# Fused forgetting attention and MLP: score tiles ahead of AV runs in batch 0, and two x transposes of batch 1 through the DMA crossbar

## The chip, the cores and the metric

The kernel runs on one core of a Trainium2 chip. The metric is the device time in microseconds of one execution. Engines are named as in the profile: PE is TensorE (PEld its weight loads), DVE is VectorE, ACT is ScalarE, POOL is GpSimd, SP is SyncE. An engine's queue is written with a q behind it: SPq issues DMAs only.

## The reference

Attention with a forget gate over 8 batches, 8 heads, 576 tokens and a head size of 64, followed by a two-layer MLP with exact GELU. All inputs and the output are float32.

```python
scores = (1 / sqrt(D)) * q @ k.T                       # per batch and head
cum    = cumsum(log(clip(f, 1e-4, 1)))                 # along the tokens
scores = where(causal, -1e9, scores + cum[:, None] - cum[None, :])
attn   = softmax(scores)
x      = (attn @ v)  -> transposed to [4608 tokens, 512]   # heads side by side
h      = x @ w_in                                      # 512 -> 2048
out    = (0.5 * h * (1 + erf(h / sqrt(2)))) @ w_out    # 2048 -> 512
```

## The kernel before

**Data.** Heads go in four pairs per batch (`HP = 4`). For each pair, `qT` and `kT` hold q and k with the 64 features of two heads on 128 partitions and 576 tokens along the free axis. The decay is folded into v: `weigh_v` (L267) multiplies v by a weight per key token (`wT`) and writes `vw` in bf16; a 65th column of weights gives the softmax's denominator. One call is one pair.

**Score tiles.** `scores(b, i, t)` (L283) computes one of four score tiles of pair i, transposed (keys on partitions), in a PSUM buffer of the pool `s_psum` (two buffers), and ScalarE exponentiates it into `e` (L313). In batch 0 and for pair 0 of batch 1 TensorE also adds the causal mask; otherwise GpSimd zeroes the masked part of `e` (L315). `attend` (L327) is an AV run: per head 15 matmuls of `e` with `vw` into an `o_psum` or `m_psum` buffer (two of each). `normalize` (L342) divides by the denominator on VectorE and writes x, tokens on partitions.

**From x to GEMM1.** GEMM1 wants x with features on partitions (`xT`). There are two ways. `to_xT` (L360) makes five TensorE transposes into PSUM and one copy by VectorE or ScalarE. `x_dma` (L372) is one DMA transpose through the crossbar, issued on SP. Before the change, batches 0 and 1 use `to_xT` for all four pairs, and later batches `x_dma`.

**From q and k to qT and kT.** Batches 0 and 1 use TensorE (`transposes_first`, L203: twelve transposes into PSUM, then a copy). Later batches use the crossbar: `transpose_dma` (L229) issues one transpose for q and one for k over four heads on SP, and `untangle` (L244) puts the result into `qT` and `kT` with eight VectorE copies a pair (L253). Batch 2's are issued in the middle of batch 1, when its q and k have landed.

**Order.** All instructions are placed by hand (`manual_schedule`): each engine runs its own in the order of the program, waits on semaphores, and nothing is reordered. `first_attention` (L581) writes out batch 0, `second_attention` (L746) batch 1, in which GEMM1 blocks that batch 0 left over (`gemm1_hold`) and the first part of GEMM2 of batch 0 (`take(fill, n)`) are put between the attention's pieces. After each attention follow GEMM1 of that batch (L819 on; there `untangle` of the next batch is put between) and, mixed into the next attention, GEMM2 in row halves (`gemm2_second` L544, `gemm2_rows` L473: PSUM banks of the pool `o_psum`, named "o", and of `m_psum`, named "m"; VectorE adds the partial sums at L561 and L513). `gemm1_begin` (L667) is the start of GEMM1 of batches 0 and 1.

**Queues.** Loads of q, k and weights, which are cast to bf16, are issued on GpSimd and stand in one order with its weighing (L272) and masking (L315). Loads of v stand on GpSimd in batches 0 and 1 and on SP later, where they share the order with crossbar transposes and stores of the output. GpSimd takes a DMA's semaphore again only when the DMA that had it eight issues before has landed.

**Batch 0 around the change.** Pair 0's v is weighed by VectorE in two instructions: key blocks 0 to 3, then block 4. The copy of `kT` of pair 3 is held back until after that (`late=True`). AV runs start as early as their operands allow: pair 0's stands ahead of score tile (2, 3), and in two stretches, row blocks 0 to 3 for both heads, then row block 4. The three w_in quarters are issued on GpSimd behind the last load of v, and GpSimd weighs pairs 2 and 3 behind them.

Of the kernel before, what the change touches and what calls it, by code (L numbers as in the profile page):

```python
# [20 lines left out]
NBLK = 5  # L21
# [32 lines left out]
def kernel(  # L54
# [10 lines left out]
    nc = tc.nc  # L65
# [25 lines left out]
    o_psum = ctx.enter_context(tc.tile_pool(name="o_psum", bufs=2, space=PSUM))  # L91
# [77 lines left out]
    def load_w_in(c):  # L169
        f4 = slice(c * d_ff // 4, (c + 1) * d_ff // 4)  # L170
        nc.gpsimd.dma_start(w_in_sb[:, :, f4], w_in_r[:, :, f4])
# [28 lines left out]
    tails = consts.tile([P, n_dm, TC], BF16)  # L200


    def transposes_first(b, i, which, pool, tag, late=False):  # L203

        src = qk_of[b][which]
        ps = pool.tile([P, JT, PT], BF16, tag=tag, name="ps_f")
        for j in range(JT):
            for h in range(2):
                nc.tensor.transpose(  # L209
                    ps[h * D : (h + 1) * D, j, :],  # L210
                    src[:, 2 * i + h, j * D : (j + 1) * D],
                    ident_bf[:PT, :PT],
                )

        dst = (qT, kT)[which][i].rearrange("d (p j) -> d p j", j=JT)
        src = ps.rearrange("d j p -> d p j")
        if late:
            return partial(nc.vector.tensor_copy, dst, src)
        if b or i:
            nc.vector.tensor_copy(dst, src)  # L220
        elif which:
            nc.vector.tensor_copy(dst[:, 0 : PT // 2], src[:, 0 : PT // 2])
            nc.scalar.copy(dst[:, PT // 2 :], src[:, PT // 2 :])
        else:
            nc.scalar.copy(dst, src)

    tq_of = {}

# [38 lines left out]
    def weigh_v(b, i, eng=nc.gpsimd, n0=0, n1=NBLK):  # L267

        hs = slice(2 * i, 2 * i + 2)
        bh = b * H + 2 * i  # L270
        w = wT[:, n0:n1, bh : bh + 2].rearrange("p n h -> p h n")
        eng.tensor_tensor(  # L272
            vw(b)[:, hs, n0:n1, 0:D],
            v_sb[:, hs, n0:n1, :],
            w.unsqueeze(3).to_broadcast([P, 2, n1 - n0, D]),
            Alu.mult,
        )
        if b:
            eng.tensor_copy(vw(b)[:, hs, :, D], w)
# [47 lines left out]
    def attend(b, i, h, ms, pool=o_psum, tag="o"):  # L327
        if (b, i, h) not in o_of:
            o_of[b, i, h] = pool.tile([P, NBLK, D + 1], FP32, tag=tag, name="o")
        o = o_of[b, i, h]  # L330
        for m in ms:
            for n in range(m + 1):
                t, c = where(n, m)
                nc.tensor.matmul(  # L334
                    o[:, m, :],
                    e_of[b, i, t][:, h, c : c + P],
                    vw_of[b][:, 2 * i + h, n, :],
                    start=(n == 0),
                    stop=(n == m),
                )  # L340

    def normalize(b, i, h):  # L342
        if (b, i) not in x_of:
            x_of[b, i] = x_pool.tile([P, NBLK, 2, D], BF16, tag="x", name="x")
        o = o_of[b, i, h]
        r = x_pool.tile([P, NBLK], FP32, tag="r", name="r")
        nc.vector.reciprocal(r, o[:, :, D])  # L347
        nc.vector.tensor_tensor(  # L348
            x_of[b, i][:, :, h, :],
            o[:, :, 0:D],  # L350
            r.unsqueeze(2).to_broadcast([P, NBLK, D]),
            Alu.mult,
        )
# [227 lines left out]
    def first_attention():  # L581


        def transposes(i, pool, tag):
            transposes_first(0, i, 0, pool, tag)
            transposes_first(0, i, 1, pool, tag)

        def attend_head(i, h, *at):
            attend(0, i, h, (0, 1, 2, 3, 4), *at)
            normalize(0, i, h)  # L590

        warm_up(9)
        transposes(0, o_psum, "o")
        nc.vector.tensor_tensor_scan(
            decay[:, S - 2 :: -1],
            f_sb[:, S - 1 : 0 : -1],
            none[:, 0 : S - 1],
            2.0**80,
            Alu.mult,
            Alu.add,  # L600
        )
        warm_up(2, 2 * P)
        scores(0, 0, 0)
        scores(0, 0, 1)
        transposes_first(0, 1, 0, m_psum, "m")
        scores(0, 0, 2)
        transposes_first(0, 1, 1, m_psum, "m")
        psw = o_psum.tile([P, NBLK, BH], FP32, tag="o", name="psw")
        for n in range(NBLK):
            nc.tensor.transpose(  # L610
                psw[:, n, :], decay[:, K0[n] : K0[n] + P], ident_fp[:BH, :BH]
            )
        scores(0, 0, 3)
        nc.vector.tensor_copy(wT[:, 0:4, :], psw[:, 0:4, :])
        nc.vector.tensor_copy(wT[D:P, 4, :], psw[D:P, 4, :])
        nc.vector.tensor_copy(
            vw(0)[:, :, :, D], wT[:, :, 0:H].rearrange("p n h -> p h n")
        )
        scores(0, 1, 0)
        transposes_first(0, 2, 0, m_psum, "m")  # L620
        scores(0, 1, 1)
        transposes_first(0, 2, 1, m_psum, "m")
        scores(0, 1, 2)
        scores(0, 1, 3)
        transposes_first(0, 3, 0, m_psum, "m")
        scores(0, 2, 0)
        copy = transposes_first(0, 3, 1, m_psum, "m", late=True)
        weigh_v(0, 0, nc.vector, 0, NBLK - 1)
        weigh_v(0, 0, nc.vector, NBLK - 1)
        copy()  # L630
        weigh_v(0, 1, nc.vector)
        load_w_in(0)
        load_w_in(1)
        load_w_in(2)
        weigh_v(0, 2)
        weigh_v(0, 3)
        load_qk_tokens(1, 0, 4)
        nc.gpsimd.memset(v_sb[:, :, 0, 0:1], 0.0)
        load_v(1, 0, 4, nc.gpsimd)
        load_w_in(3)  # L640
        load_qk_tokens(1, 4, 8)
        load_v(1, 4, 8, nc.gpsimd)
        scores(0, 2, 1)
        scores(0, 2, 2)
        for ms in ((0, 1, 2, 3), (4,)):
            for h in range(2):
                attend(0, 0, h, ms)
        for h in range(2):
            normalize(0, 0, h)
        scores(0, 2, 3)  # L650
        scores(0, 3, 0)
        for h in range(2):
            attend_head(1, h, m_psum, "m")
        scores(0, 3, 1)
        scores(0, 3, 2)
        for h in range(2):
            attend_head(2, h)
        scores(0, 3, 3)
        to_xT(0, 0, nc.vector.tensor_copy)
        to_xT(0, 1, nc.scalar.copy)  # L660
        attend_head(3, 0)
        both = s_psum.tile([P, 2, 1024], BF16, tag="s", name="ps_x2")
        to_xT(0, 2, nc.scalar.copy, ps=both[:, 0, 0:XC])
        attend_head(3, 1)
        gemm1_begin(0, both)

    def gemm1_begin(b, both):  # L667
# [78 lines left out]
    def second_attention():  # L746


        b, fill = 1, gemm2_first(0)

        def av(i, h):
            attend(b, i, h, (0, 1, 2, 3, 4))
            normalize(b, i, h)

        def transposes(i, pool, tag):
            for which in range(2):
                transposes_first(b, i, which, pool, tag)


        nc.scalar.activation(warm[0:1, 0:1], warm[0:1, 0:1], Act.Exp)  # L760
        def tiles(i, t):
            scores(b, i, t)
            scores(b, i, t + 1)

        def run(i):
            av(i, 0)
            av(i, 1)

        tiles(0, 0)
        transposes(1, o_psum, "o")  # L770
        gemm1_hold(10)
        gemm1_hold(11)
        tiles(0, 2)
        gemm1_hold(12, nc.scalar.copy)
        transposes(2, o_psum, "o")
        tiles(1, 0)
        gemm1_hold(13)
        run(0)
        tiles(1, 2)
        gemm1_hold(14, nc.scalar.copy)  # L780
        transposes(3, o_psum, "o")
        weigh_v(1, 2)
        tiles(2, 0)
        gemm1_hold(15)
        run(1)
        weigh_v(1, 3)
        tiles(2, 2)
        take(fill, 4)
        tiles(3, 0)
        transpose_dma(2, 0, 4)  # L790
        transpose_dma(2, 4, 8)
        to_xT(b, 0, nc.vector.tensor_copy, o_psum, "o")
        to_xT(b, 1, nc.vector.tensor_copy, o_psum, "o")
        take(fill, 4)
        tiles(3, 2)
        behind(qk_of[2][1], H - 1)
        load_w_out(2)
        load_w_out(3)
        run(2)
        take(fill, 4)  # L800
        av(3, 0)
        take(fill, 4)
        both = s_psum.tile([P, 2, 1024], BF16, tag="s", name="ps_x2")
        to_xT(b, 2, nc.scalar.copy, ps=both[:, 0, 0:XC])
        av(3, 1)
        gemm1_begin(1, both)
        x_tail(1)
        load_v(2)

    for b in range(B):  # L810
# [8 lines left out]
        for ffb in range(4 if b < 2 else 5, n_ff):  # L819
# [17 lines left out]
            elif b + 1 < B:  # L837
                first, gap = (5, 3) if b == 1 else (1, 4)
                at, late = divmod(ffb - first, gap)
# [40 lines left out]
```

## Time and profile before

The median of three runs is 335.3 us (334.8 to 336.39).

| | |
|---|---|
| profiled execution | 337.87 us |
| its span | 335.9 us |
| PE busy | 325.7 us (97%) |
| ACT busy | 206.6 us (61%) |
| DVE busy | 184.2 us (55%) |
| POOL busy | 133.0 us (40%) |
| granted PE clock | 1.0 throughout |
| chain that ended last | PE 90%, DMA 4%, POOL 2% |
| DMA engines busy, first 75 us | 80% or more in each slice |

How to read it: a line of a timeline is start in us, length in us, engine, line of the program, operation, and "out<-in" by names, with the number of instructions merged into it; in square brackets stands the idle time of that engine just ahead of it and what ended it. The chain is followed back from the last instruction, at each step to what released it; "issue" is time for which the profile shows no wait. A line of the DMA view's third part is queue and kind, packets, megabytes, and the time that the packets took as a share of 16 DMA engines (packets of several queues overlap, so shares above 100% occur). q0 carries the DMAs that GpSimd issues, q1 those of SP, q8 TensorE's program.

The stages, by the timeline: batch 0's attention until about 26 us, its GEMM1 until 35, batch 1's attention until 56, its GEMM1 until 70, and from 70 us on batch 2 to 7, each attention mixed with GEMM2 of the batch before.

### The profile page before, as it was taken

To read this page: it belongs to the slowest core of one execution; us is meant where nothing else is said; L and a number is where in the kernel's file an instruction comes from. 1 tells how busy PE (TensorE), PEld (TensorE's weight loads), DVE (VectorE), ACT (ScalarE), POOL (GpSimd) and SP (SyncE) were. 2 spreads that over 40 slices of the span, in tenths; PEclk is the share of its full clock that TensorE was granted. 3 is DMA by queue.
4 is the path that set the end of the run, shared out by engine and by line. 5 is a ranking of instruction groups with operands and counts; after the bars stand their busy time and mean duration, and the time that the engine had idled before them with its cause. 6 is when DMAs were issued, how large, how long until landed. Compare 5 with 4: busy or idle time off the path is not lost.

```text
span 335.9 us, 7819 instructions
## 1 busy us (share of the span) xinstructions
PE 325.7 (97%) x3161; PEld 170.7 (51%) x3161; DVE 184.2 (55%) x424; ACT 206.6 (61%) x298; POOL 133.0 (40%) x260
## 2 busy tenths in 40 slices
PE   7779999999999999999999999999999999999995
PEld 3564555445554456445644555446544654444443
DVE  5671666594358945894579547964696550020011
ACT  4957886983734787378827882788378846404600
POOL 8787874029437044723445344525441420000000
PEclk9999999999999999999999999999999999999999
DMA  8999998999998799599947995769800231011012
GB/s 117 188 187 219 194 189 116 158 181 158 207 205 175 120 204 185 102 140 149 212 128 108 170 195 157 112 119 192 195 13 2 87 72 49 0 72 54 0 45 81
DMA packets 97427, 44.16 MB, mean 131 GB/s; under 512 B 75728, under 2 KB 92368, under 8 KB 97392
## 3 DMA queue, kind: packets, MB, share of 16 engines
q1 hardware_dynamic: 79344, 27.55, 41.6%
q0 software_dynamic: 17648, 15.60, 30.5%
q8 instruction: 24, 0.39, 0.5%
q10 hardware_dynamic: 400, 0.52, 0.4%
q14 instruction: 11, 0.09, 0.1%
HBM read 36.85 MB, written 9.44 MB: 138 GB/s over the span
## 4 chain that ended last, share of the span: by engine, by line
PE 90%; DMA 4%; POOL 2%; issue 1%; DVE 1%; ACT 0%; POOLq 0%; ACTq 0%
PE ps L389 36%; PE ps L493 26%; PE o L334 9%; PE ps L433 8%; PE s L303 7%; DMA v_sb<-in_v_dram 2%; DMA xT<-x 1%; PE ps L553 1%; PE ps_x L367 1%; PE ps L529 1%; PE ps_f L209 1%; POOL k L109 1%; POOL q L109 1%; DVE vw L272 0%; ACT e L313 0%
## 5 line engine op out<-in xcount | busy, mean ns | idle before, releaser
L409 ACT ACTIVATE g<-ps 128x512 bf16<-128x512 f32 x138 | 78.5, 601 | 79.8 <-PE ps L389 79.3
L313 ACT ACTIVATE e<-s 128x896 bf16<-128x896 f32 (+2 forms) x128 | 100.2, 835 | 23.8 <-PE s L303 18.7
L389 PE MATMUL ps<-xT,w_in_sb 128*128 128x512 bf16 x512 | 113.6, 379 | 0.1
L493 PE MATMUL ps<-w_out_sb,g 64*128 64x512 bf16 (+1 forms) x711 | 108.0, 377 | 0.0
L389 PEld LDWEIGHTS <-w_in_sb 128*128 128x128 bf16 x576 | 55.5, 98 | 67.4 <-issue 3.1
L315 POOL TENSOR_SCALAR_AFFINE_SELECT e<-e 128x256 bf16<-128x256 bf16 (+1 forms) x135 | 49.1, 383 | 90.1 <-ACT e L313 89.9
L493 PEld LDWEIGHTS <-g 64*128 64x128 bf16 (+1 forms) x711 | 39.4, 95 | 34.7 <-issue 4.2
L272 POOL TENSOR_TENSOR vw<-v_sb,wT 128x640 bf16<-128x640 f32 x30 | 38.7, 1290 | 26.1 <-DMA v_sb<-in_v_dram 15.3
L303 PE MATMUL s<-qT,kT 64*128 64x320 bf16 (+4 forms) x384 | 42.9, 276 | 1.5 <-ACT e L313 0.7
L253 DVE COPY kT<-tk 64x288 bf16<-64x288 bf16 x96 | 42.8, 446 | 1.6
L253 DVE COPY qT<-tq 64x288 bf16<-64x288 bf16 x96 | 40.0, 417 | 5.1 <-DMA tq<-q 3.7
L334 PEld LDWEIGHTS <-e 128*128 128x128 bf16 x960 | 34.7, 98 | 9.6 <-POOL e L315 2.9
L501 DVE COPY ot<-ps 128x512 f32<-128x512 f32 x20 | 13.8, 692 | 46.5 <-PE ps L493 46.5
L334 PE MATMUL o<-vw,e 128*128 128x65 bf16 x960 | 37.1, 194 | 1.3 <-DVE vw L272 1.3
L348 DVE TENSOR_TENSOR x<-o,r 128x320 bf16<-128x320 f32 x64 | 31.5, 492 | 3.1 <-DVE r L347 0.7
L442 DVE COPY ot<-ps 128x512 f32<-128x512 f32 (+2 forms) x9 | 5.7, 632 | 49.6 <-PE ps L433 49.6
L303 PEld LDWEIGHTS <-kT 64*128 64x128 bf16 x384 | 19.2, 94 | 21.5 <-issue 4.8
L433 PE MATMUL ps<-w_out_sb,g 128*128 128x512 bf16 (+2 forms) x144 | 28.0, 355 | 0.0
L433 PEld LDWEIGHTS <-g 128*128 128x128 bf16 x144 | 13.5, 98 | 14.5
L347 DVE RECIPROCAL r<-o 128x5 f32<-128x5 f32 x64 | 12.1, 188 | 11.3 <-PE o L334 11.3
L513 DVE TENSOR_TENSOR ot<-ot,ps 128x512 f32<-128x512 f32 x22 | 15.1, 685 | 1.1
L389 PE MATMUL ps<-tails,w_in_sb 128*128 128x512 bf16 x64 | 14.3, 378 | 0.0
(69 smaller groups left out, 153.6 us busy)
## 6 DMA issues: line engine op xcount, KB each, us to landing
out_dram<-ot SPq DMA_DIRECT2D x32, 256.0 KB, 2.4
v_sb<-in_v_dram SPq DMA_DIRECT2D x24, 256.0 KB, 4.8
q<-in_q_dram POOLq DMA_DIRECT2D x6, 576.0 KB, 6.3
k<-in_k_dram POOLq DMA_DIRECT2D x6, 576.0 KB, 8.4
w_in_sb<-in_moe_w_in_dram POOLq DMA_DIRECT2D x4, 512.0 KB, 8.0
w_out_sb<-in_moe_w_out_dram POOLq DMA_DIRECT2D x4, 512.0 KB, 9.2
v_sb<-in_v_dram POOLq DMA_DIRECT2D x13, 128.0 KB, 7.1
v_sb<-in_v_dram SPq DMA_DIRECT2D x9, 128.0 KB, 4.7
```

Of the source, the lines that this page charges most:

```text
L253: nc.vector.tensor_copy(rows[:, odd], src[odd * D : (odd + 1) * D, 2 * i + h].rearrange("d j p -> d p j"),)
L272: eng.tensor_tensor(vw(b)[:, hs, n0:n1, 0:D], v_sb[:, hs, n0:n1, :], w.unsqueeze(3).to_broadcast([P, 2, n1 - n0, D]), Alu.mult,)
L303: nc.tensor.matmul(to, *ab, start=half < 0, stop=half == 1 or not masked)
L313: nc.scalar.activation(et[:, :, z:c], st[:, :, z:c], Act.Exp, scale=scale)
L315: nc.gpsimd.affine_select(out=et[:, :, c0 + z : c0 + P], in_=et[:, :, c0 + z : c0 + P], compare_op=Alu.is_ge, fill=0.0, base=z, pattern=[[ ...
L334: nc.tensor.matmul(o[:, m, :], e_of[b, i, t][:, h, c : c + P], vw_of[b][:, 2 * i + h, n, :], start=(n == 0), stop=(n == m),)
L348: nc.vector.tensor_tensor(x_of[b, i][:, :, h, :], o[:, :, 0:D], r.unsqueeze(2).to_broadcast([P, NBLK, D]), Alu.mult,)
L389: nc.tensor.matmul(ps, w_in_sb[:, kt, ffb * P : (ffb + 1) * P], src[:, kt, 0:TC], start=(kt == 0), stop=(kt == n_dm - 1),)
L409: nc.scalar.activation(g_of[c][ffb], ps, Act.Gelu)
L433: nc.tensor.matmul(pss[ts][:, c0:c1], g_of[c][kt][:, ts * P : (ts + 1) * P], w_out_sb[:, kt, c0:c1], start=(kt == 0), stop=(kt == n_ff - 1),)
L493: nc.tensor.matmul(banks[r], g_of[c][kt][rows, ts * P : (ts + 1) * P], w_out_sb[rows, kt, :], start=kt == (steps.index("r") if r else 0), ...
L513: nc.vector.tensor_tensor(ot, ot, bank, Alu.add)
```

## The change

In batch 0:

- the first qT copy is shared by VectorE and ScalarE as the first kT copy is, instead of ScalarE alone;
- the copy of kT of pair 3 is no longer held back;
- pair 0's v is weighed by GpSimd in one instruction, behind the issue of w_in quarter 0 and ahead of the issue of quarters 1 and 2;
- score tiles (2, 3), (3, 1) and (3, 3) stand ahead of the AV runs of pairs 0, 1 and 2 instead of behind them, and pair 0's AV run goes head by head in one stretch, with its `normalize` behind each head;
- xT of pair 0 is copied by ScalarE instead of VectorE;
- the second head of pair 3's AV run stands ahead of the transposes of pair 2's x instead of behind them.

In batch 1:

- x of pairs 0 and 1 goes through `x_dma`, right behind the AV run of each, instead of `to_xT` later (ten TensorE transposes and two VectorE copies). On SP the two stand ahead of batch 2's `transpose_dma`.

```diff
-    def transposes_first(b, i, which, pool, tag, late=False):
+    def transposes_first(b, i, which, pool, tag):
...
-        if late:
-            return partial(nc.vector.tensor_copy, dst, src)
         if b or i:
             nc.vector.tensor_copy(dst, src)
-        elif which:
+        else:
             nc.vector.tensor_copy(dst[:, 0 : PT // 2], src[:, 0 : PT // 2])
             nc.scalar.copy(dst[:, PT // 2 :], src[:, PT // 2 :])
-        else:
-            nc.scalar.copy(dst, src)
...
-        copy = transposes_first(0, 3, 1, m_psum, "m", late=True)
-        weigh_v(0, 0, nc.vector, 0, NBLK - 1)
-        weigh_v(0, 0, nc.vector, NBLK - 1)
-        copy()
+        transposes_first(0, 3, 1, m_psum, "m")
+        load_w_in(0)
+        weigh_v(0, 0)
         weigh_v(0, 1, nc.vector)
-        load_w_in(0)
         load_w_in(1)
         load_w_in(2)
         weigh_v(0, 2)
...
         scores(0, 2, 1)
         scores(0, 2, 2)
-        for ms in ((0, 1, 2, 3), (4,)):
-            for h in range(2):
-                attend(0, 0, h, ms)
+        scores(0, 2, 3)
         for h in range(2):
-            normalize(0, 0, h)
-        scores(0, 2, 3)
+            attend_head(0, h)
         scores(0, 3, 0)
+        scores(0, 3, 1)
         for h in range(2):
             attend_head(1, h, m_psum, "m")
-        scores(0, 3, 1)
         scores(0, 3, 2)
+        scores(0, 3, 3)
         for h in range(2):
             attend_head(2, h)
-        scores(0, 3, 3)
-        to_xT(0, 0, nc.vector.tensor_copy)
+        to_xT(0, 0, nc.scalar.copy)
         to_xT(0, 1, nc.scalar.copy)
         attend_head(3, 0)
+        attend_head(3, 1)
         both = s_psum.tile([P, 2, 1024], BF16, tag="s", name="ps_x2")
         to_xT(0, 2, nc.scalar.copy, ps=both[:, 0, 0:XC])
-        attend_head(3, 1)
         gemm1_begin(0, both)
...
         gemm1_hold(13)
         run(0)
+        x_dma(b, 0)
         tiles(1, 2)
...
         gemm1_hold(15)
         run(1)
+        x_dma(b, 1)
         weigh_v(1, 3)
         tiles(2, 2)
         take(fill, 4)
         tiles(3, 0)
         transpose_dma(2, 0, 4)
         transpose_dma(2, 4, 8)
-        to_xT(b, 0, nc.vector.tensor_copy, o_psum, "o")
-        to_xT(b, 1, nc.vector.tensor_copy, o_psum, "o")
         take(fill, 4)
```

## The prediction

> **What bounds the kernel now.** I read the page first, then the chain of waits piece by piece from 20 to 60 us, the timelines of SP, VectorE and TensorE around the two places of the edit, and last the DMA view in short windows. The page says that TensorE is busy nearly throughout:
>
> ```profile
> PE 325.7 (97%) x3161; PEld 170.7 (51%) x3161; DVE 184.2 (55%) x424; ACT 206.6 (61%) x298; POOL 133.0 (40%) x260
> ```
>
> So only what lengthens TensorE's own work or makes it wait counts; from 57 us on the chain is TensorE without a gap, and what is lost or won before that reaches the end undiminished. The chain in order of time (start, length, what) shows the two places that the edit touches:
>
> ```profile
> 22.79 0.17 PE ps_x L367 x3
> 22.96 1.62 issue
> 24.58 0.27 PE ps_x L367 x2
> ...
> 49.99 0.66 PE ps_x L367 x10
> ```
>
> The 0.66 us at 49.99 are the ten transposes of x of pairs 0 and 1 of batch 1, on the path. The 1.62 us of "issue" stand in the middle of five transposes, with no data to wait for. The DMA view tells more: a queue of kind "instruction" moves 16 KB packets, one per about 252 matmuls and weight loads of TensorE (25 for 6322). Packet times put one at 14.3 us and the next at 22.1 us, and TensorE stops after its 702nd such instruction. Counting back 252, it passed the previous boundary at 17.15 us, in the first AV run. I read this as: passing a boundary asks for the next block but one, and here it came 7.4 us later (4.95 us until its packet started, 0.9 us for it, 1.6 us after it).
>
> SP's and VectorE's timelines show a second clock, that of the DMA:
>
> ```profile
> 50.35 1.36 SPq L239 DMA_TRANSPOSE tq<-q  x1
> 53.24 1.31 SPq L239 DMA_TRANSPOSE tk<-k  x1
> 54.59 2.13 SPq L239 DMA_TRANSPOSE tq<-q  x1
> 56.76 6.73 SPq L239 DMA_TRANSPOSE tk<-k  x1
> ```
>
> ```profile
> 67.07 1.34 DVE L253 COPY qT<-tq 64x288 bf16<-64x288 bf16 x4 [3.68 <-DMA tq<-q]
> 71.13 1.34 DVE L253 COPY kT<-tk 64x288 bf16<-64x288 bf16 x4
> 72.51 0.69 DVE L561 TENSOR_TENSOR ot<-ot,ps 128x512 f32<-128x512 f32 x1
> 73.23 0.69 DVE L513 TENSOR_TENSOR ot<-ot,ps 128x512 f32<-128x512 f32 x1
> ```
>
> ```profile
> 74.23 1.89 PE L493 MATMUL ps<-w_out_sb,g 64*128 64x512 bf16 x16
> ```
>
> Batch 2's q and k are transposed by the crossbar once they have landed (50.35 and 53.24). VectorE sits idle 3.68 us until the third of these transposes has landed (67.07), untangles until 72.47, and only then adds up the first GEMM2 sums, until 73.92. That frees the two "o" banks that TensorE takes at 74.23. The margin is 0.31 us.
>
> **Part A: batch 0.** The first qT copy moves from one ScalarE copy (0.64 us) to halves on VectorE (0.46) and ScalarE (0.40). In the trace the second half of the first kT copy waits for the first half; if both pairs do so, the first exponential starts about 0.16 us later, or 0.2 earlier if not. ScalarE's 0.22 us gap at 14.69, set by k's landing, takes that: zero.
>
> kT of pair 3 (VectorE, 0.75 us) goes ahead of the weighing, into idle time: zero.
>
> The weighing of pair 0 goes from VectorE (0.69 + 0.30 us, done at 16.99) to GpSimd (1.28 us by its row). It waits for the last of pair 0's v, which VectorE saw at 16.69, so it ends at 17.97. Behind it on GpSimd stand the issues of w_in quarters 1 and 2, then at 15.79 and 16.95, now near 18.0 and 18.75; then the weighings of pairs 2 and 3 (18.53 to 21.05, now 19.5 to 22.0) and batch 1's loads (20.99, now 22.0). The packets of w_in quarter 0 end at 19.25 and a quarter's data start 1.4 us after its issue, so quarter 1 starts at 19.4: the DMA stream hardly breaks, and the gates that follow (27.10 to 30.34 us, all on landings) stay.
>
> TensorE had pair 0's AV at 16.33 to 17.3; it now does the score tile (2,3) first, waits about 1.9 us, and runs AV at 18.0 to 19.0. ScalarE's exponentials, which ended at 22.25, then end near 22.85: tile (3,0) comes 1 us later than before, and the tiles that now run ahead of AV make good most of it. Copying xT of pair 0 on ScalarE (0.69) for VectorE (0.48) makes ScalarE's two copies end at 24.2 instead of 22.9, still before GEMM1 reads them. So TensorE reaches the block boundary, now in the last AV run of pair 3, at about 23.8 instead of 22.7. From there the work is the same (12 AV matmuls and 5 transposes for 15 and 2).
>
> What decides is when the block comes. The boundary before it, passed in the same AV run, is passed 1.6 us later, at 18.75. With the same 7.4 us the block is there at 26.2, 1.6 us later than before. If the request meets a shorter queue, since w_in quarters 1 and 2 are issued later, there is no stall, and TensorE goes on at 23.8: 0.8 us earlier. Part A: -0.8 to +1.6 us. The other latencies from boundary to packet, up to 57 us, were 4.1, 3.6 (from the end of the stall), 1.1, 3.1 and 1.7 us, so I take neither end, but +0.4.
>
> [...]
>
> One more cost of moving the weighing: pair 1's weighing stays on VectorE (0.82 us) and waits for the same v. What the two engines do to each other shows where GpSimd weighs beside untangling:
>
> ```profile
> 102.49 1.79 DVE L253 COPY qT<-tq 64x288 bf16<-64x288 bf16 x2
> ```
>
> Two copies that take 0.67 us elsewhere take 1.79 here: one waited for GpSimd. If GpSimd waits instead, AV starts 0.82 us later, w_in too, and the DMA stream breaks for up to 0.8 us. I count zero and keep 0.8. [...]
>
> **Part B: batch 1.** Removed are ten transposes (0.66 us of the path) and two VectorE copies (0.89 us, not on the path). What follows on TensorE then waits for exponentials that end at 51.14 instead of starting late, so I count -0.5.
>
> Added are two crossbar transposes on SP. They are ahead of batch 2's four on that queue; the second can go once x of pair 1 is normalized, 48.72, so SP itself is free again at 49.95, before 50.35. The transfers are not free:
>
> ```profile
> q0 software_dynamic: 1316, 1.00, 130.0%
> ```
>
> That is the DMA view from 45 to 50 us: the 16 engines are full with batch 2's q and k, the loads that release the transposes. One x has 128 x 640 x 2 bytes, 640 packets of 256 bytes. Their price alone and in a mix, from the windows 264 to 266 us (x by itself) and 61 to 65 us (transposes beside w_out):
>
> ```profile
> q1 hardware_dynamic: 672, 0.16, 36.4%
> ```
>
> ```profile
> q0 software_dynamic: 616, 0.61, 91.2%
> q1 hardware_dynamic: 613, 0.16, 31.5%
> ```
>
> 0.364 x 16 x 2 us / 672 = 17 ns a packet; 0.315 x 16 x 4 / 613 = 33 ns. So one x costs each engine 640/16 x 17 to 33 ns, 0.7 to 1.3 us, and two 1.4 to 2.6 us. Above that, transposes stick in busy queues: of those begun at 86.5 us many end only at 88.2, 1.7 us later, all at once. With 1.5 us of this each the two cost 5.6. I take 2.6, the mix being the nearest row. If the later load (k, 53.24) lands that much later, so does everything behind it on SP and VectorE: the untangling starts at 69.7, the sums are added by 76.5, and TensorE gets its banks 2.3 us after 74.23. If VectorE frees them after TensorE is ready, TensorE's own shift (0.4 - 0.5 = -0.1) does not matter: the later one sets the time. v of batch 2 lands at 76.1 instead of 73.5; GpSimd's chain to the AV run at 81.7 has moved by as much as TensorE.
>
> **Sum.** max(-0.1, 2.6 - 0.31) = +2.3 us. The profiled execution took 337.87 us (span 335.9), 2.6 above the median of 335.3; I carry the difference over: 335.3 + 2.3 = 337.6 us.
>
> **Rivals.**
> 1. Not slower: the transposes hide. If x of pair 0 is through before the last loads and the slowest of the 16 engines is not one that it slows, k lands as before, and the untangling's margin lets TensorE gain 0.31 at most where part A helps, while a late block leaves 1.6 - 0.5 = +1.1. For it: k's last two engines land at 53.1, 1.5 us behind the others. Against: every engine gets its share of a transpose. It decides below a delay of 0.3 us. 335.0 to 336.4 us.
> 2. Faster: the block comes before it is wanted, and q and k of batch 2 come earlier as well: -0.8 - 0.5 = -1.3 us or a little more, 333.6 to 334.0. Nothing in the profile shows what would bring them earlier.
> 3. x itself is late: x of pair 1, issued at 48.75, must land by 55.4 for GEMM1 of batch 1. With the slowest landing of an x (4.8 us) it is there at 53.6; with the slowest of a transpose in the mix (11.3 us) at 60.05, and TensorE waits 4.6 us: 339.9. For it: 130% load at the time.
>
> **How the numbers follow.** About 0.5% (1.7 us) is what a measurement of this kernel can tell from no change. The forecast's case 0.55, of which 0.45 lie above 1.7 us (own range 336.6 to 339.0); rival 1 0.25; rival 2 0.08, nearly all of it inside 1.7 us but for what is unknown; rival 3 0.12, above. So slower 0.57, within 0.36, faster 0.07. Eight in ten: from 335.0 (rival 2 and the lower edge of rival 1 left out) to 340.2 (rival 3 taken in, the 5.6 us of sticking left out).
>
> **What would show it.** Right: tq of batch 2 issued after 51 us, tk after 54.5, VectorE's idle time before L253 longer and ending near 69.7, and a wait of TensorE at L493 for VectorE's L513 near 74 us. For part A: weighing by GpSimd until 18.0 to 18.8, an "issue" gap of 1 to 3 us inside pair 3's AV run, or none. Wrong: tk issued at 53.2 as before, or TensorE waiting near 55 us for xT from DMA. The forecast falls if the two transposes take less than 0.3 us from the loads, or if the block fetch moves by more than 2 us.

## The result, and the profile after

The changed kernel takes 338.8 us (median of six runs, 338.24 to 339.95), the kernel before beside it 335.29. The ratio is 1.0101, with a 95% interval of 1.0078 to 1.0124: 3.5 us slower. The profiled execution took 338.24 us with a span of 336.5 us. Most lines of the new file stand four below those of before: the AV run is now L330, the weighing L268, untangling L249, the sums L557 and L509, GEMM2's row halves L489.

The page of the changed kernel: busy times, granted clock, and the chain by engine.

```profile
PE 323.0 (96%) x3110; PEld 171.9 (51%) x3151; DVE 182.5 (54%) x420; ACT 206.7 (61%) x299; POOL 135.8 (40%) x261
...
PEclk9979999999999999999999999999999999999998
...
PE 74%; DMA 13%; POOL 7%; DVE 2%; issue 2%; SPq 0%; ACT 0%; POOLq 0%; ACTq 0%
```

Three things are new. The granted clock has a 7 in its third slice (16.8 to 25.2 us), where it was full before. The chain no longer is TensorE from 57 us on: 13% of it are DMA now. And the "issue" stall of 1.62 us, which the prediction let decide part A, is gone.

**Batch 0.** GpSimd's, TensorE's and ScalarE's timelines of the changed kernel:

```profile
15.70 1.93 POOL L268 TENSOR_TENSOR vw<-v_sb,wT 128x640 bf16<-128x640 f32 x1 [0.71 <-DMA v_sb<-in_v_dram]
```

```profile
17.68 1.81 PE L330 MATMUL o<-vw,e 128*128 128x65 bf16 x30 [1.51 <-POOL vw L268]
```

```profile
20.34 3.27 ACT L309 ACTIVATE e<-s 128x896 bf16<-128x896 f32 x4 [3.21 <-PE s L299]
```

The weighing took 1.93 us, not the 1.28 of its row. TensorE waited 1.51 us for it, and then its AV run took 1.81 us, where the same 30 matmuls took 1.11 in the first profile of the kernel before, behind a gap of 1.14 us:

```profile
16.33 1.11 PE L334 MATMUL o<-vw,e 128*128 128x65 bf16 x30 [1.14 <-DVE vw L272]
```

Here are the windows of that stretch in the changed kernel; the last three columns are the granted clock, the DMA share and GB/s:

```profile
16.00:17.00 1.00, 0.16 (x6) 0.11 (x2) 0.49 (x1) 1.00 (x2) 1.00 (x1) 1.00 0.71 105
17.00:18.00 1.00, 0.32 (x7) 0.32 (x7) 0.00 (x0) 0.12 (x1) 1.00 (x2) 0.50 1.21 196
18.00:19.00 1.00, 1.00 (x23) 1.00 (x20) 0.27 (x2) 0.00 (x0) 1.00 (x2) 0.50 1.16 193
19.00:20.00 1.00, 1.00 (x19) 0.83 (x18) 0.86 (x3) 0.00 (x0) 0.99 (x2) 0.50 0.49 82
20.00:21.00 1.00, 1.00 (x27) 0.75 (x23) 0.24 (x1) 0.66 (x1) 1.00 (x2) 0.79 1.16 183
```

While TensorE stood, its granted clock went down to 0.5 and stayed there until 20.4 us. ScalarE, which lives from the score tiles, idled 3.21 us. By its busy share, 1.00 from 18 to 20 us, this TensorE at a clock of 0.50 looks like any busy TensorE; the clock column tells it, and the length of its rows (1.81 us instead of 1.11).

**Batch 1.** SP's and VectorE's timelines, and the chain in order of time:

```profile
44.31 6.00 SPq L369 DMA_TRANSPOSE xT<-x  x2
51.06 2.07 SPq L235 DMA_TRANSPOSE tq<-q  x1
54.72 1.42 SPq L235 DMA_TRANSPOSE tk<-k  x1
```

```profile
67.17 1.35 DVE L249 COPY qT<-tq 64x288 bf16<-64x288 bf16 x4 [2.63 <-DMA tq<-q]
...
73.35 0.69 DVE L509 TENSOR_TENSOR ot<-ot,ps 128x512 f32<-128x512 f32 x1
```

```profile
40.43 14.28 DMA k<-in_k_dram
...
56.19 10.96 DMA tq<-q
...
73.35 0.70 DVE ot L509
74.05 0.04 issue
74.09 3.66 PE ps L489 x31
```

The chain now runs from k's landing through the crossbar's tq to VectorE's untangling and sums, and TensorE joins it at 74.09, where the predicted gate stands. By how much it gates could not be read from these two profiles: the first profile of the kernel before was itself 2.6 us longer than its median.

### The profile page after: what moved, and what is told of

It is laid out like the page before. It is cut to its first block, busy times and chain, and to the rows that moved or that the text cites. A ratio compares the mean times of both kernels' runs of the same rounds, so it can differ in the third digit from the quotient of the medians.

```text
span 336.5 us, 7764 instructions
## 1 busy us (share of the span) xinstructions
PE 323.0 (96%) x3110; PEld 171.9 (51%) x3151; DVE 182.5 (54%) x420; ACT 206.7 (61%) x299; POOL 135.8 (40%) x261
## 4 chain that ended last, share of the span: by engine, by line
PE 74%; DMA 13%; POOL 7%; DVE 2%; issue 2%; SPq 0%; ACT 0%; POOLq 0%; ACTq 0%
PE ps L385 28%; PE ps L489 25%; PE ps L429 8%; PE o L330 7%; DMA k<-in_k_dram 7%; PE s L299 5%; DMA tq<-q 3%; POOL v_sb L121 2%; POOL vw L268 2%; DMA v_sb<-in_v_dram 1%; DMA xT<-x 1%; POOL q L109 1%; DVE kT L249 1%; DVE qT L249 1%; POOL k L109 1%
## 5 line engine op out<-in xcount | busy, mean ns | idle before, releaser
L385 PE MATMUL ps<-xT,w_in_sb 128*128 128x512 bf16 x495 | 112.3, 379 | 1.2 <-DMA xT<-x 0.2
L489 PE MATMUL ps<-w_out_sb,g 64*128 64x512 bf16 (+1 forms) x692 | 104.8, 376 | 1.7 <-issue 1.3
L489 PEld LDWEIGHTS <-g 64*128 64x128 bf16 (+1 forms) x711 | 40.2, 95 | 34.8 <-issue 4.7
L268 POOL TENSOR_TENSOR vw<-v_sb,wT 128x640 bf16<-128x640 f32 x31 | 40.6, 1313 | 26.6 <-PE s L299 16.0
L249 DVE COPY kT<-tk 64x288 bf16<-64x288 bf16 x96 | 46.0, 480 | 3.3 <-DMA tk<-k 1.7
L299 PE MATMUL s<-qT,kT 64*128 64x320 bf16 (+4 forms) x384 | 44.2, 278 | 2.1 <-ACT e L309 1.5
L330 PEld LDWEIGHTS <-e 128*128 128x128 bf16 x960 | 35.1, 99 | 9.6 <-issue 3.0
L330 PE MATMUL o<-vw,e 128*128 128x65 bf16 x960 | 37.5, 195 | 2.3 <-POOL vw L268 1.5
L249 DVE COPY qT<-tq 64x288 bf16<-64x288 bf16 x96 | 36.7, 382 | 4.0 <-DMA tq<-q 2.6
L299 PEld LDWEIGHTS <-kT 64*128 64x128 bf16 x384 | 20.0, 94 | 22.4 <-issue 6.1
L509 DVE TENSOR_TENSOR ot<-ot,ps 128x512 f32<-128x512 f32 x22 | 15.1, 685 | 1.1
```

Source lines behind the costliest of these rows:

```text
L249: nc.vector.tensor_copy(rows[:, odd], src[odd * D : (odd + 1) * D, 2 * i + h].rearrange("d j p -> d p j"),)
L268: eng.tensor_tensor(vw(b)[:, hs, n0:n1, 0:D], v_sb[:, hs, n0:n1, :], w.unsqueeze(3).to_broadcast([P, 2, n1 - n0, D]), Alu.mult,)
L299: nc.tensor.matmul(to, *ab, start=half < 0, stop=half == 1 or not masked)
L330: nc.tensor.matmul(o[:, m, :], e_of[b, i, t][:, h, c : c + P], vw_of[b][:, 2 * i + h, n, :], start=(n == 0), stop=(n == m),)
L385: nc.tensor.matmul(ps, w_in_sb[:, kt, ffb * P : (ffb + 1) * P], src[:, kt, 0:TC], start=(kt == 0), stop=(kt == n_dm - 1),)
L489: nc.tensor.matmul(banks[r], g_of[c][kt][rows, ts * P : (ts + 1) * P], w_out_sb[rows, kt, :], start=kt == (steps.index("r") if r else 0), ...
```

## The experiments

All were timed in five rounds. Ratios are to the kernel before, with 95% intervals.

**1. The kernel before, once more** (e0_before_again; no edit).

> The kernel before, unchanged, for a second profile of it. Its first profiled execution took 337.87 us, 2.6 us above the median of its runs, so that profile may hold stalls that most executions do not have. If so (theory S), the new profile is near 335.3 us, the 1.62 us of 'issue' inside x's transposes near 23 us is gone or much shorter, and the DMA packets that stood still from 58.8 to 60.85 us do not. If the 2.6 us are only what profiling adds (theory P), the same stalls show and the execution again takes about 338 us.

Measured: 335.61 us, 1.0013 [0.9997, 1.0029]; span of the profile 333.7 us. The 1.62 us stall isn't in it: TensorE's timeline has no "issue" gap from 14 to 27 us, and the third slice of GEMM1 began at 23.89 us instead of 26.43. SP's and VectorE's timelines of this run, in which the sums are done at 71.5 and TensorE waits for neither:

```profile
52.19 2.43 SPq L239 DMA_TRANSPOSE tk<-k  x1
```

```profile
64.64 1.34 DVE L253 COPY qT<-tq 64x288 bf16<-64x288 bf16 x4 [1.18 <-DMA tq<-q]
```

So the stall belonged to one execution, and this profile (span 333.7, 335.64 us) is the one to compare with.

**2 and 3. Each part alone.** e1_batch0_alone is the changed kernel with batch 1 as before; e2_batch1_alone is the kernel before with

```diff
         run(0)
+        x_dma(b, 0)
...
         run(1)
+        x_dma(b, 1)
...
-        to_xT(b, 0, nc.vector.tensor_copy, o_psum, "o")
-        to_xT(b, 1, nc.vector.tensor_copy, o_psum, "o")
```

> The changed kernel with batch 1 as before (x of pairs 0 and 1 of batch 1 by TensorE, two VectorE copies): part A alone. Theory B (the loss is the crossbar's, in batch 1): within 0.4 us of the kernel before. Theory A (the loss is batch 0's: the first AV run waits for GpSimd's weighing, TensorE idles 1.5 us, the granted clock falls to 0.5 for some 3 us, and the block of program that came late in the first profile of the kernel before is not late in most executions): 2.5 to 4 us slower, with part B worth -0.6 to +1.

> The kernel before with the two crossbar transposes of x in batch 1 instead of ten TensorE transposes and two VectorE copies: part B alone. Theory B, as predicted: +2.3 us or more, with VectorE untangling batch 2's later half 2 us later and TensorE waiting for VectorE's sums near 74 us. Theory A: between -0.6 us (what TensorE saves) and +1 us.

Measured: part A alone 337.89 us, 1.0077 [1.0051, 1.0104], 2.6 us; part B alone 336.55 us, 1.0049 [1.0024, 1.0075], 1.2 us. Together 3.8, and the whole change costs 3.5. The medians nearly add, but the interval of the whole change, 2.6 to 4.2 us, begins where part A alone stands; and in the profiles batch 2's first AV run starts at 79.19 us in experiment 1, at 81.93 with part A, 80.45 with part B and 81.59 with both, so there both cost no more than part A. Part A's profile shows the same late weighing, with VectorE's weighing beside it, and then the AV run:

```profile
15.88 0.83 DVE L268 TENSOR_TENSOR vw<-v_sb,wT 128x640 bf16<-128x640 f32 x1 [0.70 <-DMA v_sb<-in_v_dram]
15.92 1.93 POOL L268 TENSOR_TENSOR vw<-v_sb,wT 128x640 bf16<-128x640 f32 x1 [1.35 <-DMA v_sb<-in_v_dram]
```

```profile
17.89 1.81 PE L330 MATMUL o<-vw,e 128*128 128x65 bf16 x30 [1.79 <-POOL vw L268]
```

VectorE's weighing of pair 1 waits for v as well, starts 0.04 us earlier and takes its usual time; GpSimd's takes 0.65 us more than its 1.28. VectorE's operation still had 0.79 us to run when GpSimd's began, so the extra 0.65 us are nearly what GpSimd would lose by waiting for it. That it waits is read from these rows; what the two engines share, a port in the expectations below, no run shows. Which of the two starts first is called the race from here on.

Part B's SP, VectorE and TensorE timelines:

```profile
41.98 6.05 SPq L373 DMA_TRANSPOSE xT<-x  x2
50.07 1.80 SPq L239 DMA_TRANSPOSE tq<-q  x1
53.54 2.12 SPq L239 DMA_TRANSPOSE tk<-k  x1
```

```profile
66.05 1.35 DVE L253 COPY qT<-tq 64x288 bf16<-64x288 bf16 x4 [0.95 <-DMA tq<-q]
```

```profile
53.91 0.81 PE L389 MATMUL ps<-xT,w_in_sb 128*128 128x512 bf16 x3 [0.54 <-DMA xT<-x]
...
72.24 0.37 PE L493 MATMUL ps<-w_out_sb,g 64*128 64x512 bf16 x1 [0.18 <-DVE ot L561]
72.96 1.88 PE L493 MATMUL ps<-w_out_sb,g 64*128 64x512 bf16 x15 [0.35 <-DVE ot L513]
```

Against experiment 1, k's transpose is issued 1.35 us later and the untangling starts 1.41 us later. TensorE then waits 0.18 us for one bank at L493 and 0.35 for the other. Ahead of the banks it is 0.21 us behind experiment 1 (a score tile starts at 71.70 instead of 71.49), behind them 1.26 (the AV run at 80.45 instead of 79.19). The mechanism is the predicted one; its size is half. But TensorE also waits 0.54 us for x of pair 1, which comes at 53.9 us. That is the third rival in small, and it takes back the 0.5 us that the ten transposes would have saved.

**4. The changed kernel with pair 0 weighed on VectorE** (e3_weigh_on_vector).

```diff
-        weigh_v(0, 0)
+        weigh_v(0, 0, nc.vector)
```

> The changed kernel with one edit undone: pair 0's v is weighed by VectorE (in one instruction) instead of GpSimd; score tiles stay ahead of the AV runs, the crossbar stays. Theory A in the form 'the weighing does it': the first AV run starts near 17.0 us instead of 17.7, TensorE's gap before it falls from 1.5 to under 1 us, w_in quarters 1 and 2 are issued near 15.7 and 16.9 again, and 1 to 2.5 us of the 3.5 come back. If the order of tiles and runs does it, it stays 2.5 to 3.5 us slower than before; by theory B too.

Measured: 336.87 us, 1.0051 [1.0032, 1.0069], 1.5 us over the kernel before: about 2 of the 3.5 us are gone with this one word. TensorE's timeline:

```profile
16.67 1.11 PE L330 MATMUL o<-vw,e 128*128 128x65 bf16 x30 [0.67 <-DVE vw L268]
```

The gap is 0.67 us and the clock 1.0 throughout. 1.5 less part B's 1.2 leaves 0.3 us for the rest of part A, mainly the order of the tiles; in the profile TensorE passes the same weight load (the 400th) 1.05 us later than in experiment 1, 0.42 of it in an "issue" stall (at 23.07) ahead of pair 3's last 12 AV matmuls, where the prediction had put the block boundary. So that rest costs 0.3 to 1 us.

**5. Part A with the gap filled** (e4_gap_filled): seven matmuls of zeros, which take no part in the result, behind score tile (2, 3).

```diff
         scores(0, 2, 3)
+        warm_up(7)
         for h in range(2):
             attend_head(0, h)
```

> Part A alone (batch 0's changes) with seven matmuls of zeros, 0.216 us each, put on TensorE between score tile (2,3) and the first AV run; they take no part in the result. Part A alone was 2.56 us slower than before; in its profile TensorE idles 1.79 us ahead of the first AV run, then runs 3 us at a granted clock of 0.5 (AV run 1.81 us instead of 1.11, the tiles behind it 1.13 instead of 0.66). Theory 'clock': with the gap filled the grant stays at 1.0, 0.8 to 1.4 us come back, and the kernel is 1.2 to 1.8 us slower than before. Theory 'wait': only the late start counts; the kernel stays 2.3 to 2.8 us slower, whatever the grant does.

Measured: 337.2 us, 1.0063 [1.0041, 1.0085]. The weighing still took 1.92 us, AV began at 17.66 us (17.89 in part A alone), but took 1.11 us, and the clock stayed at 1.0. TensorE reaches the third slice of GEMM1 at 25.37 us instead of 26.62; with the 0.23 us of the earlier start taken off, the clock was worth some 1.0 us of part A there. In the medians it is 0.7 us (337.89 to 337.2), by the ratios 0.5, with intervals that overlap. By its ratio this kernel is 2.1 us slower than before, between the ranges of the two theories, so the clock's share is read from these rows and not decided by the time.

**6 and 7. Part B with a part of the untangling moved behind the sums** (e5_batch1_alone_sums_first), and the kernel before with the same edit (e6_before_sums_first):

```diff
                 take(fill, counts[i][t])
+                if b == 2 and (i, t) == (0, 1):
+                    untangle(2, 3)
...
-                if late == 0:
+                if late == 0 and not (b == 1 and at == 3):
                     untangle(b + 1, at)
```

> Part B alone (two crossbar transposes of x) with one more edit: untangling of pair 3 of batch 2 (eight VectorE copies, 2.7 us) moved behind the first two pairs of GEMM2 sums, so that the sums no longer wait for it. Part B alone was 1.2 us slower than before. Theory 'gate' (the late transposes cost time only because the sums that free TensorE's banks stand behind the untangling on VectorE): the 1.2 us go and TensorE's saving of 0.5 us shows: between 0.6 us faster and 0.1 us slower than before. Theory 'queue' (the late DMAs hurt elsewhere, v of batch 2 and GpSimd's chain behind it): still 0.8 us or more slower.

> The kernel before with the same move of pair 3's untangling and nothing else, the control for the run above. In the second profile of the kernel before, the sums were done 0.2 us before TensorE wanted the banks, so it should be the same within 0.3 us; if the margin is mostly missed in other executions, up to 0.5 us faster.

Measured: 341.72 us, 1.0194 [1.0167, 1.0221], and 339.83 us, 1.0141 [1.0108, 1.0174]. Both much slower, against what was expected. VectorE's timeline of e5_batch1_alone_sums_first, and TensorE's:

```profile
72.24 0.69 DVE L513 TENSOR_TENSOR ot<-ot,ps 128x512 f32<-128x512 f32 x1
...
74.74 3.43 DVE L253 COPY qT<-tq 64x288 bf16<-64x288 bf16 x4
78.18 6.03 DVE L253 COPY kT<-tk 64x288 bf16<-64x288 bf16 x4
84.24 0.69 DVE L501 COPY ot<-ps 128x512 f32<-128x512 f32 x1
```

```profile
84.98 1.81 PE L334 MATMUL o<-vw,e 128*128 128x65 bf16 x30 [3.92 <-DVE ot L501]
```

In the control, VectorE and GpSimd:

```profile
75.17 5.02 DVE L253 COPY kT<-tk 64x288 bf16<-64x288 bf16 x4
```

```profile
75.99 1.27 POOL L272 TENSOR_TENSOR vw<-v_sb,wT 128x640 bf16<-128x640 f32 x1
```

The gate itself went: the first sums wait for TensorE there, 0.56 us, and not it for them. But the eight moved copies, 2.7 us elsewhere, took 9.5 us (7.1 in the control). They now stand beside GpSimd's weighings and masking of batch 2, which keep their usual length; that this is the cause is read from the rows and was not tested. TensorE waited 3.92 us for the sums behind them (1.57 in the control), its AV run then took 1.81 us (1.59) instead of 1.11, and the mean granted clock of both profiled executions is 0.995, from which an estimate (0.005 of their spans of 340.9 and 337.0 us, twice) makes some 3.4 us at 0.5. The place of the untangling matters more than the gate that it makes, and the times do not tell the two theories apart. The difference between the two runs, 1.9 us, is not the gate's price: TensorE is 1.66 us behind the control already ahead of the sums that wait for the moved copies (a score tile at 73.20 instead of 71.54), and most of that is one wait for x of pair 1:

```profile
55.41 0.81 PE L389 MATMUL ps<-xT,w_in_sb 128*128 128x512 bf16 x3 [1.38 <-DMA xT<-x]
```

**8 and 9. Only the weighing on GpSimd** (e7_weigh_on_gpsimd_alone and, unchanged, e11_weigh_on_gpsimd_again): the kernel before, with the order of tiles and AV runs as it was. The copy of kT of pair 3 is no longer held back here either.

```diff
-        weigh_v(0, 0, nc.vector, 0, NBLK - 1)
-        weigh_v(0, 0, nc.vector, NBLK - 1)
         copy()
-        weigh_v(0, 1, nc.vector)
         load_w_in(0)
+        weigh_v(0, 0)
+        weigh_v(0, 1, nc.vector)
         load_w_in(1)
```

> The kernel before with one part of part A: pair 0's v weighed by GpSimd in one instruction, behind the issue of w_in quarter 0 (the copy of pair 3's kT, no longer held back, goes with it); order of tiles and AV runs as before. If the weighing is the cause by itself: 2 to 3 us slower than before, TensorE idle over 2 us ahead of the first AV run, granted clock 0.5 behind it, the weighing near 1.9 us instead of 1.28 because VectorE weighs pair 1 at the same time. If the order of tiles and AV runs is the larger part: under 1.2 us slower.

> The kernel before with only pair 0's weighing on GpSimd, once more, unchanged, for another profile. Theory 'port race and clock': the runs fall in two groups again, near 336 us with a mean clock of 0.998 or more and near 339 us with 0.99 to 0.995; a profile of the second group shows GpSimd's weighing at 1.9 us instead of 1.28, a gap of TensorE of 1.5 us or more ahead of AV and a granted clock of 0.5 for about 3 us behind it. Rival: a profile near 339 us without those three.

Measured: 339.01 us, 1.0099 [1.0067, 1.0130], and 338.64 us, 1.0080 [1.0052, 1.0108]. The seventeen runs spread from 335.9 to 340.32 us. Those with a mean granted clock of 0.997 or more are at 335.9 to 337.6 us (four), those below at 338.46 to 340.32 (thirteen). The expected second group was there, though the two lie closer than 336 and 339. The two profiles fell on either side. The first (335.9 us), GpSimd, VectorE and TensorE:

```profile
14.74 1.28 POOL L272 TENSOR_TENSOR vw<-v_sb,wT 128x640 bf16<-128x640 f32 x1 [0.74 <-DMA v_sb<-in_v_dram]
...
14.87 1.83 DVE L272 TENSOR_TENSOR vw<-v_sb,wT 128x640 bf16<-128x640 f32 x1
...
16.08 1.11 PE L334 MATMUL o<-vw,e 128*128 128x65 bf16 x30 [0.84 <-POOL vw L272]
```

and the second (339.68 us):

```profile
15.83 0.83 DVE L272 TENSOR_TENSOR vw<-v_sb,wT 128x640 bf16<-128x640 f32 x1 [0.53 <-DMA v_sb<-in_v_dram]
15.86 1.93 POOL L272 TENSOR_TENSOR vw<-v_sb,wT 128x640 bf16<-128x640 f32 x1 [1.69 <-DMA v_sb<-in_v_dram]
...
17.84 1.81 PE L334 MATMUL o<-vw,e 128*128 128x65 bf16 x30 [2.27 <-POOL vw L272]
```

The same program, twice: where GpSimd starts first, it takes 1.28 us and VectorE's weighing 1.83; where VectorE starts 0.03 us earlier, it is 0.83 and 1.93. In the second TensorE stands 2.27 us, and the clock is at 0.5 from 16.5 to 23.3 us, as these of its windows show:

```profile
16.00:17.00 1.00, 0.00 (x0) 0.00 (x0) 0.65 (x1) 0.58 (x1) 1.00 (x1) 0.74 1.20 206
17.00:18.00 1.00, 0.16 (x4) 0.16 (x4) 0.00 (x0) 0.00 (x0) 1.00 (x2) 0.50 1.22 200
...
22.00:23.00 1.00, 1.00 (x20) 0.80 (x19) 0.83 (x4) 0.00 (x0) 1.00 (x2) 0.50 1.25 205
```

It is not the race alone that makes the 2.27 us: v also landed about 1.1 us later in the second. Part A's own runs divide in the same way: two with a clock of 0.999 at 336.2 us, six with 0.99 to 0.995 at 337.8 to 339.7. One run of the whole change, however, had a mean clock of 1.0 and still took 338.54 us, so the clock is not all of it in each run. The kernel before has single runs at a lower clock too, three on record: 337.04 and 337.09 us at 0.993 and 339.01 us at 0.977.

**10 and 11. The race taken out** (e8_batch0_alone_port_apart, on part A, and e9_gpsimd_port_apart, on the kernel of experiment 8). Of the first:

```diff
         weigh_v(0, 0)
-        weigh_v(0, 1, nc.vector)
...
         for h in range(2):
             attend_head(0, h)
+        weigh_v(0, 1, nc.vector)
```

> Part A alone, with VectorE's weighing of pair 1 moved behind pair 0's normalization, so that GpSimd weighs pair 0 with nothing of VectorE beside it. Theory 'port race and clock' (the weighing took 1.93 us instead of 1.28 because VectorE's weighing of pair 1 held it up; TensorE then stood 1.8 us and its granted clock fell to 0.5): the weighing takes 1.28 us, AV starts 0.65 us earlier than in part A alone, TensorE's gap ahead of it is about 1.1 us, the granted clock stays at 1.0 from 17 to 21 us, and the price falls from 1.0077 to about 1.003 to 1.0045 (the order of the tiles alone: +1.0 to +1.5 us). Rival 'GpSimd is late in any case' (the queue of w_in quarters and weighings behind it is what costs): as part A alone, 1.0065 to 1.009.

> The kernel before with only pair 0's weighing on GpSimd (which alone gave 1.0099, runs of 335.9 and of 338.5 to 339.7 us), and VectorE's weighing of pair 1 moved behind pair 0's normalization. Theory 'port race and clock': no run holds the race any more, so all runs lie near the one in which GpSimd had won it: 335.5 to 336.5 us, ratio 1.000 to 1.003, mean granted clock 0.997 or more in each. Rival: 1.008 to 1.012 as with the race.

The edit was at fault: in program order the weighing of pair 1 now stands behind the load of batch 1's v into the same buffer, so it waited for that load (11.87 us of idle time on VectorE in the first) and weighed batch 1's values for batch 0. The times, 350.47 and 352.36 us, say nothing on the question, and it stays untimed. Only the stretch up to pair 0's AV run can be read. GpSimd and TensorE in the first:

```profile
15.57 1.28 POOL L268 TENSOR_TENSOR vw<-v_sb,wT 128x640 bf16<-128x640 f32 x1 [1.57 <-DVE kT L218]
...
16.91 1.11 PE L330 MATMUL o<-vw,e 128*128 128x65 bf16 x30 [0.75 <-POOL vw L268]
```

and TensorE in the second:

```profile
17.33 1.11 PE L334 MATMUL o<-vw,e 128*128 128x65 bf16 x30 [2.08 <-POOL vw L272]
```

With nothing of VectorE's beside it the weighing takes 1.28 us in both, as the theory had it. But in the second TensorE stood 2.08 us, v having landed late, and the granted clock stayed at 1.0 until 22.8 us. So the length of the gap alone does not decide whether the clock falls.

**12. Part B for x of pair 0 alone** (e10_batch1_one_x).

```diff
         run(0)
+        x_dma(b, 0)
...
-        to_xT(b, 0, nc.vector.tensor_copy, o_psum, "o")
         to_xT(b, 1, nc.vector.tensor_copy, o_psum, "o")
```

> Part B for x of pair 0 alone; x of pair 1 through TensorE as before. Theory 'every transpose delays the loads of q and k by its packets' time, and the margin of 0.2 to 0.3 us is used up first': k of batch 2 lands 0.6 to 0.7 us later than before (1.35 with both), VectorE's untangling starts 0.7 us later, TensorE saves 0.33 us: +0.1 to +0.6 us, ratio 1.0003 to 1.002. Rival 'only x of pair 1, issued among the last of the loads, delays them': no delay, and the 0.33 us saved on TensorE show as -0.3 to 0 us, 0.999 to 1.000. Rival 'the first one does it all': +1.0 to +1.4 us, 1.003 to 1.0045.

Measured: 335.76 us, 1.0001 [0.9973, 1.0029]. SP's and VectorE's timelines:

```profile
41.61 1.37 SPq L373 DMA_TRANSPOSE xT<-x  x1
...
52.41 2.32 SPq L239 DMA_TRANSPOSE tk<-k  x1
```

```profile
64.88 1.34 DVE L253 COPY qT<-tq 64x288 bf16<-64x288 bf16 x4 [1.95 <-DMA tq<-q]
```

k's transpose is issued 0.22 us later than in experiment 1 and the untangling starts 0.24 us later, a sixth of what both x cost, not half. The rival that the first does it all is out; between the other two the interval does not decide, and the 0.24 us lie nearer to the one that blames x of pair 1. No version tried beats the kernel before.

## Why the prediction was right, and where not

The forecast was 337.6 us in a range of 335.0 to 340.2; 338.8 were measured. The sign and the size came out, but the parts did not: part B was put too high by about 1.1 us, part A too low by about 2.2 (it cost 2.6, outside its own range of -0.8 to +1.6). In the sum part A counted for nothing, and it is the larger of the two. That the total still came within 1.2 us is luck: the two errors have opposite signs.

- **"Sum. max(-0.1, 2.6 - 0.31) = +2.3 us."** The larger term was the wrong one: TensorE's own shift, put at -0.1, is some 2 us (part A's 2.6 less the 0.5 saved), and part B, put at 2.3, is 1.2. Whether the two meet in a maximum or add (2.6 and 1.2, together 3.5) the medians leave open; the AV runs of the profiles speak for the maximum. But the max held TensorE's shift and the loads apart, and a later batch 0 also issues x and the loads later. The two x transposes went at 44.31 instead of 41.98, the load of k at 40.43 instead of 39.19, and the untangling started at 67.17 (both parts), 66.05 (B) and 64.64 (neither): with the crossbar transposes in place, A's delay moves the gate too. Without them it does not: in part A alone k's transpose was issued at 52.21, in experiment 1 at 52.19.
- **Part B's gate** is shown: SP's tk at 54.72 (forecast: after 54.5), tq after 51, VectorE's untangling late, the wait at L489, where TensorE joins the chain at 74.09. What failed is "I take 2.6, the mix being the nearest row": k came 1.35 us later, just under the 1.4 of the lower bound, at 17 ns a packet, which was the lower end of the same step. The sixth found with one x (0.22 us of 1.35) says that the price isn't a fixed time per transpose either; whether it depends on when the transpose meets the loads was not shown.
- **Part A, "What decides is when the block comes."** It did not. The stall was a property of the one execution that the prediction was read from; it was absent from the second profile of the same kernel, and from that of the changed one. The 7.4 us from boundary to block were taken as a property of the kernel.
- **"I count zero and keep 0.8"** for the two weighings' conflict: this is the step of part A that failed. GpSimd lost in four of the five profiles in which both engines waited for the same v, and its weighing then took 0.64 to 0.65 us more. With the time at which v lands this sets whether TensorE stands 0.84 us or 1.5 to 2.3.
- **"AV at 18.0 to 19.0"**: it began at 17.68 and took 1.81 us. The half clock behind the gap was in none of the prediction's steps. In experiment 5 filling the gap gave some 1.0 us of TensorE's time back, and experiment 4 gives about 2 us for the weighing's place with all that follows.
- **The base.** The prediction subtracted 2.6 us from the profiled execution and added the effects worked out from its rows. The stall of 1.62 us was most of those 2.6, so what the sum let the change do to it (from -0.8 to +1.6) was done to something that the median does not hold.
- **Rivals.** Transposes that hide: out by experiment 3, though nearly right for one x. Faster: out. x itself late for GEMM1 of batch 1: not in the changed kernel, in whose groups only 0.2 us are counted for TensorE behind xT, but in small in experiments 3 and 6 (0.54 and 1.38 us near 54 us), and the prediction had named this wait as a sign that it was wrong.

What stays open is what decides whether the clock falls: the gaps after which it fell (1.51, 1.57, 1.79, 2.27 and 3.92 us) and after which it did not (0.58 to 1.14, 1.38, 1.62 and 2.08) overlap. What losing the race costs was not timed apart from the clock either, and the 0.3 to 1 us of the rest of part A have no experiment of their own.

## What to carry to other kernels

Profile the kernel before twice before a stall in it is made a term of a sum: here a 1.6 us stall was one execution's. When two engines are set on operations that wait for the same load, as the two weighings were, count the price of losing the race (here 1.93 us instead of 1.28), plus what the engine behind them does with a gap: here TensorE ran at half its clock for 3.4 to 6.8 us, and its busy share of 1.00 does not show it. Two crossbar transposes beside loads that were waited for put k's transpose 1.35 us back here, and the first of them alone 0.22, so look for a place where no load is waited for.

## What the runs showed of the hardware that was not expected

- The granted clock fell 0.8 to 1.1 us after TensorE had stopped ahead of the first AV run (stopped at 16.16, 16.11 and 15.57 us, fallen at 17.0, 17.25 and 16.5 by windows of a quarter of a microsecond) and came back 3.4, 3.4 and 6.8 us after the fall. The shortest stop after which it fell was 1.51 us. In experiments 6 and 7, after 3.92 and 1.57 us, the low clock lasted some 3.4 us too, by the estimate from the mean clock of 0.995.
- Eight small bf16 copies of VectorE, 2.7 us by themselves, took 7.1 and 9.5 us beside GpSimd's weighings and masking.
- The same program lost or won the race by 0.03 to 0.13 us in the order of two starts, and its runs lie up to 4.4 us apart (335.9 to 340.32).
